# Weight preparation spread over more steps in a kernel that runs attention and a gated MLP side by side

## The chip, the cores and the metric

The kernel runs on one core of one Trainium2 chip. The core has five engines with queues of their own: TensorE (PE in the profile, with PEld for its weight loads), VectorE (DVE), ScalarE (ACT), GpSimd (POOL) and SyncE (SP, which here issues all DMAs). The metric is the device time of one execution in microseconds; the span in a profile goes from the first to the last instruction and is a little shorter.

## The reference

One block of a model on 2048 tokens of width 640. The layer-normed input goes two ways, and the product of the two is added to the input:

```python
def _A_ref(x, wqkv, wo):                  # sliding-window attention, H = 32 heads of 20, W = 256
    q, k, v = split(x @ wqkv)
    scores = einsum("bhqd,bhkd->bhqk", q, k) * (Dh ** -0.5)
    mask = (i - j >= 0) & (i - j < W)
    p = softmax(where(mask, scores, -1e9))
    return (p @ v).reshape(B, S, D) @ wo

def _B_ref(x, w1, b1, w2, b2):            # F = 1536
    h = x @ w1 + b1
    r = where(h > 0, h, 0)
    return (r * r) @ w2 + b2

xn = _layernorm(x)
return x + _A_ref(xn, wqkv, wo) * silu(_B_ref(xn, w1, b1, w2, b2))
```

(shortened; the shapes are x 2048x640, wqkv 640x1920, wo 640x640, w1 640x1536, w2 1536x640, all float32.)

## The kernel before

Every float32 factor of a dense product is split into two float16 parts, a high and a low one, after scaling by a power of two; a product is then three matmuls (high by high, high by low, low by high). To find the scale of a weight its squares are summed first. So each weight is loaded twice: once for squares (ACT, line 792, `unread<-raw`), once for the split, which takes one ACT instruction for the high part (line 126) and one DVE instruction for the low part (line 127).

The program has three parts. First, layer norm, transposes, the value product and the first group of 128 columns of q and k. Last, the product with wo, the gate and the residual. Between them lies the long middle part, to which nearly all of the change belongs: a loop over steps, written out by hand, so that each engine runs its instructions in the order in which the loop emits them.

A **step** of the middle part handles 128 queries of one pair of heads (16 pairs of 16 steps, 256 steps, and 13 more that only drain). In it stand, for different positions of a pipeline: `scores` (four matmuls into `sps`, line 574) and their running maxima on DVE (`junk`, line 585); ten steps later `scores_t` (four matmuls into `stps`, line 621), the exponential on ACT (`p`, line 626) and two masks on POOL (lines 627 and 629); one step later the high part of the probabilities on ACT (`ph`, line 634); one more step later the low part on DVE (`pl`, line 640); and at last 24 matmuls per two steps with the values (`ops`, line 654). There is a single PSUM tile for `stps`, so the next `scores_t` waits until the exponential has read the last one; likewise the next `scores` waits until the maxima have read both tiles of `sps`.

Into each step `fill` puts a fixed amount of **dense products**, reckoned in planned microseconds: 0.35 of it before and 0.65 of it after the middle of the step. The amount, `per`, is the planned total of 423.5 us divided by 268 steps, 1.58 us. The products come from a list of units:

- `group_unit`: q and k for groups 1 to 4 of 128 columns, 32 units of 15 matmuls of 512 columns (`qkps`, line 705), each evacuated by one ACT and one DVE instruction (lines 81 and 82);
- `hidden_unit`: the MLP's hidden layer, 96 units of 15 matmuls of 256 columns (`hps`, line 705), each evacuated by two ACT instructions (864 and 865), one on DVE (867) and one on POOL (868);
- `out_unit`: the MLP's second product, 96 units of 12 matmuls of 320 columns (`yps`, line 890); it needs w2 split.

The first 16 group units stand alone, the other 16 are merged with the 12 hidden units of the first block of 256 rows; then hidden units of one block and out units of the block before alternate.

The weights that the middle part prepares (q and k columns of the next group, the squares of w2 and wo, the splits of w2, the splits of wo) are **pieces** in one queue, first in, first out. `start_pieces` issues a piece's load on SP, at most three held at once; `release` emits its work on ACT and DVE, at most one piece a step, and not sooner than two steps after its load (`AGE`). `ensure` emits what is left of a kind at once. Evacuations are emitted by `flush` in the middle of a step.

## Time and profile before

| | |
|---|---|
| time, median of 3 runs (lowest to highest) | 834.24 us (833.88 to 835.12) |
| profiled execution: time, span | 834.25 us, 832.5 us |
| granted TensorE clock | 1.00 |
| PE, DVE, ACT, POOL busy | 815.6, 686.8, 646.7, 476.5 us |
| middle part: first `sps` matmul, last exponential | 117.2 us, 748.3 us |

Busy time of PE is to be read with care: a matmul's record lasts longer than the time after which the next can start (a record of 273 ns, but 15 matmuls in 1.64 us), so PE can look busy where it waits. What PE achieves is better read from counts: how many steps, four `sps` matmuls each, fall into a stretch of time. The records of DMA-issuing instructions show when SP issues them, not when the data lands.

### The profile page before, as it was taken

The numbers are of one execution on the slowest core, as the hardware profiler recorded it, in microseconds if no ns is written. First come the engines' busy times: TensorE is split into PE (matmuls) and PEld (weight loads), VectorE is DVE, ScalarE is ACT, GpSimd is POOL, SyncE is SP. The second block draws the span as 40 slices with busy tenths as digits, with TensorE's granted clock in tenths as the row PEclk, the third lists the DMA queues.
The fourth block names the chain that finished last, engine by engine and source line by source line (L and its number), as shares of the span: only waits on it lengthen the run. The fifth ranks groups of instructions, "written<-read, shape, count | busy, mean of one in ns | idle before, by whom it ended". The sixth has DMA issues, their size and how long they took to land.

```text
span 832.5 us, 24962 instructions
## 1 busy us (share of the span) xinstructions
PE 815.6 (98%) x9453; PEld 548.6 (66%) x9453; DVE 686.8 (82%) x1903; ACT 646.7 (78%) x1024; POOL 476.5 (57%) x874
## 2 busy tenths in 40 slices
PE   8999999999989999999999999999999999999998
PEld 7776553445555557777777777777777777767776
DVE  6777566788999889888988889888988889875665
ACT  4565446998898989898898989898898989893321
POOL 2000001456776778787877878787887878771000
PEclk9999999999999999999999999999999999999999
DMA  6895348765563332212121212212231231055883
GB/s 241 258 342 163 118 134 275 223 192 157 150 200 108 108 90 74 64 37 66 54 77 46 67 49 54 65 52 50 55 88 34 67 98 46 10 200 181 303 297 129
DMA packets 100641, 104.51 MB, mean 126 GB/s; under 512 B 42536, under 2 KB 73000, under 8 KB 100520
## 3 DMA queue, kind: packets, MB, share of 16 engines
q1 hardware_dynamic: 100520, 102.91, 40.4%
q8 instruction: 74, 1.21, 0.6%
q14 instruction: 47, 0.39, 0.2%
HBM read 65.67 MB, written 36.83 MB: 123 GB/s over the span
## 4 chain that ended last, share of the span: by engine, by line
PE 82%; ACT 7%; DVE 6%; issue 3%; DMA 2%; SPq 0%; DVEq 0%; ACTq 0%
PE hps L705 19%; PE yps L890 19%; PE wops L705 8%; PE ops L654 7%; PE qkps L705 7%; PE sps L574 7%; PE vps L293 6%; PE stps L621 3%; PE qkps L519 3%; ACT p L626 2%; DVE junk L585 1%; DVE pl L640 1%; ACT ph L634 1%; PE otp L972 1%; DMA raw<-in_B_w_dram 1%
## 5 line engine op out<-in xcount | busy, mean ns | idle before, releaser
L626 ACT ACTIVATE p<-stps,ebias,esc 128x768 f32<-128x768 f32 (+2 forms) x256 | 242.3, 946 | 50.0 <-PE stps L621 42.3
L585 DVE CUSTOM_DVE_ANT_0 junk<-sps,mask 128x320 bf16<-128x320 f32 (+2 forms) x512 | 221.5, 469 | 54.7 <-PE sps L574 44.3
L640 DVE TENSOR_TENSOR pl<-p,ph 128x768 f16<-128x768 f32 (+2 forms) x256 | 243.4, 951 | 4.8 <-ACT ph L634 4.1
L627 POOL TENSOR_SCALAR_AFFINE_SELECT p<-p 128x256 f32<-128x256 f32 x256 | 171.5, 670 | 90.4 <-ACT p L626 87.6
L634 ACT ACTIVATE ph<-p 128x768 f16<-128x768 f32 (+2 forms) x256 | 203.1, 793 | 2.1 <-POOL p L629 1.2
L705 PE MATMUL hps<-xT,w 128*128 128x256 f16 x1440 | 188.8, 273 | 0.0
L890 PE MATMUL yps<-w,hh 128*128 128x320 f16 x1152 | 186.6, 300 | 0.0
L705 PEld LDWEIGHTS <-w 128*128 128x128 f16 x1440 | 133.2, 98 | 43.7 <-issue 23.7
L890 PEld LDWEIGHTS <-hh 128*128 128x128 f16 x1152 | 105.1, 98 | 55.6 <-issue 21.8
L705 PE MATMUL qkps<-xT,qkw 128*128 128x512 f16 x480 | 117.0, 380 | 0.8 <-DVE w_t L154 0.8
L629 POOL TENSOR_SCALAR_AFFINE_SELECT p<-p 128x256 f32<-128x256 f32 x224 | 110.6, 494 | 0.0
L574 PE MATMUL sps<-ks,qs 60*64 60x320 f16 (+2 forms) x1024 | 86.0, 313 | 6.3 <-DVE mt L585 5.7
L654 PE MATMUL ops<-vp,ph 128*128 128x41 f16 x1440 | 89.8, 181 | 0.0
L654 PE MATMUL ops<-vp,pl 128*128 128x41 f16 x1440 | 89.5, 180 | 0.0
L654 PEld LDWEIGHTS <-ph 128*128 128x128 f16 x1440 | 84.5, 96 | 6.2 <-issue 0.6
L654 PEld LDWEIGHTS <-pl 128*128 128x128 f16 x1440 | 78.9, 96 | 5.8
L621 PE MATMUL stps<-qs,ks 62*64 62x320 f16 (+4 forms) x1024 | 79.6, 291 | 2.1 <-ACT p L626 1.8
L590 POOL CAST mp<-mt 128x8 f16<-128x8 f32 x64 | 44.0, 688 | 62.2 <-DVE mt L585 61.5
L705 PEld LDWEIGHTS <-qkw 128*128 128x128 f16 x480 | 41.6, 98 | 53.5 <-issue 11.7
L868 POOL TENSOR_TENSOR hh<-sq,hh 128x256 f16<-128x256 f32 x96 | 67.6, 704 | 13.0 <-DVE sq L867 9.3
L293 PE MATMUL vps<-wv,xT 128*128 128x320 f16 x480 | 69.6, 299 | 1.3 <-DVE xT L267 0.4
L705 PE MATMUL wops<-wo,oT 128*128 128x320 f16 (+1 forms) x495 | 66.7, 295 | 0.8 <-ACT oT L122 0.8
(152 smaller groups left out, 975.9 us busy)
## 6 DMA issues: line engine op xcount, KB each, us to landing
ks<-k_d SPq DMA_DIRECT2D x64, 120.0 KB
qs<-q_d SPq DMA_DIRECT2D x64, 120.0 KB
raw<-in_B_w_dram SPq DMA_DIRECT2D x24, 320.0 KB
v_d<-vt SPq DMA_DIRECT2D x8, 656.0 KB
vp<-v_d SPq DMA_DIRECT2D x16, 328.0 KB
xt<-in_A_x_dram SPq DMA_DIRECT2D x16, 320.0 KB
k_d<-shm SPq DMA_DIRECT2D x20, 256.0 KB
q_d<-shm SPq DMA_DIRECT2D x20, 256.0 KB
```

Of the source, the lines that this page charges most:

```text
L293: nc.tensor.matmul(ps, xT[b][:, xp, c, t * P:(t + 1) * P], wv[wp][:, c, nh * HALF:(nh + 1) * HALF], start=n == 0, stop=n == 3 * KC - 1)
L574: nc.tensor.matmul(ps[HB * j:HB * (j + 1), :nk], qs[i][rows_, q0:q0 + HB], ks[i][rows_, k0:k0 + nk], start=True, stop=True)
L585: nc.vector.tensor_tensor_reduce(out=junk[:, :nk], in0=ps[:, :nk], in1=mk, scale=1.0 / MAX_UNIT, scalar=-3.0e38, op0=ALU.add, op1=ALU.max, ...
L621: nc.tensor.matmul(ps[HB * j:HB * (j + 1), hh, c0:c1], ks[i][rows_, kb * P + HB * j:kb * P + HB * (j + 1)], qs[i][rows_, kb * P + c0:kb * ...
L626: nc.scalar.activation(p32[:, :, :n], ps[:, :, :n], AF.Exp, scale=esc[0], bias=ebias)
L627: nc.gpsimd.affine_select(p32[:, :, 0:P], p32[:, :, 0:P], pattern=[[0, 2], [1, P]], compare_op=ALU.is_ge, fill=0.0, base=0, channel_multip ...
L629: nc.gpsimd.affine_select(p32[:, :, 2 * P:], p32[:, :, 2 * P:], pattern=[[0, 2], [-1, P]], compare_op=ALU.is_gt, fill=0.0, base=0, channel ...
L634: nc.scalar.activation(ph[:, :, :n], p32[:, :, :n], AF.Copy)
L640: nc.vector.tensor_sub(pl[:, :, :n], p32[:, :, :n], ph[:, :, :n])
L654: nc.tensor.matmul(ot[:, q % 4, hh, :], t[:, hh, (q - k) * P:(q - k + 1) * P], vp[:, k // 4, k % 4, hh, :], start=m == 1, stop=m == 2 * le ...
L705: nc.tensor.matmul(ps, a, b_, start=j == 0, stop=j == n - 1)
L890: nc.tensor.matmul(ps, hh[:, hp, tt * P:(tt + 1) * P], lin1(w2t, (2 * fc + wp) * D + nh * HALF, HALF), start=fc == 0 and j == 0, stop=fc = ...
```

## The change

Seven edits, all in the order in which the middle part emits its work. The set of products, of their evacuations, of loads and of splits is the same.

1. **Pace.** `release` now also waits for a distance since the last piece of the same kind: 2 or 3 steps for splits of w2 (in turn), 2 steps for squares once the exponentials have begun (after step 11), 1 step for all else.
2. **Squares from the first unit on.** The 17 squares are queued when group 1 begins, not two units later. The loads for the next group of q and k are queued one unit later than before, and ahead of the squares that still wait in the queue; the `shut` flag that held them back is gone.
3. **12 per cent more dense products** in each of the first 72 steps: 1.77 planned us instead of 1.58; each later step gets 1.51, so that the total is the same.
4. **Merging begins earlier**: hidden units are mixed in after 12 group units, not 16.
5. **The scale of wo** is worked out by a function of its own, before the third hidden unit of the second block, not together with the scale of w2.
6. **The first turn moved**: the transposes of the first 256 rows of the attention's output (`otp`, then `oT`) are emitted before the last-but-one out unit, if their load has been issued, not after the last.
7. `transposes` is moved out of `out_filler` for that; its text is unchanged.

```diff
--- before.py
+++ after.py
@@ -734,6 +734,13 @@
     AGE = 2
     held = [0]
     shut = set()
+    last = {}
+
+    def pace(kind):
+        if kind == "2":
+            return 2 + len(w2t) % 2
+        return 2 if kind == "s" and state[2] > LAG + 1 else 1
+
 
     def start_pieces(n=3):
         k = 0
@@ -748,8 +755,9 @@
         done = []
         while started and len(done) < n:
             tag, at_, go = started[0]
-            if not force and (tag in shut or state[2] < at_ + AGE):
+            if not force and (tag in shut or state[2] < at_ + AGE or state[2] < last.get(tag[0], -9) + pace(tag[0])):
                 break
+            last[tag[0]] = state[2]
             done.append(started.pop(0)[2])
         return done
 
@@ -766,21 +774,24 @@
                 f()
                 held[0] -= 1
 
-    def piece(tag, src, go):
+    def piece(tag, src, go, ahead=False):
         def start():
             raw = wgt.tile([P, D], F32, tag="wraw", bufs=RAW, name="raw")
             if len(src.shape) == 3:
                 raw = raw.rearrange("p (c n) -> p c n", n=src.shape[-1])
             nc.sync.dma_start(raw, src)
             return lambda: go(raw)
-        queue.append((tag, start))
+        if ahead:
+            queue.insert(sum(t == tag for t, _ in queue), (tag, start))
+        else:
+            queue.append((tag, start))
 
     def queue_group(g):
         r = {}
         for i, w in enumerate("qk"):
             hi, lo = (qkw[0][:, g % 2, i, j] for j in range(2))
             off = (0 if w == "q" else D) + g * P
-            piece(f"g{g}", wqkv.rearrange("(c p) n -> p c n", p=P)[:, :, off:off + P], lambda raw, hi=hi, lo=lo, w=w: split_s(hi, lo, raw, sc_g[w]))
+            piece(f"g{g}", wqkv.rearrange("(c p) n -> p c n", p=P)[:, :, off:off + P], lambda raw, hi=hi, lo=lo, w=w: split_s(hi, lo, raw, sc_g[w]), True)
             r[w] = (hi, lo)
         return r
 
@@ -799,13 +810,16 @@
 
     def second_scales():
         s2, i2 = weight_scale("w2", totals("w2_t", pmm.tile([P, NF], F32, tag="mm", name="sums2"), mlp["g2"]))
-        so, io = weight_scale("wo", totals("wo_t", pmm.tile([P, KC], F32, tag="mm", name="sumso"), sso))
         sf = col("m_sf", NF)
         nc.vector.tensor_scalar(sf, mlp["ic2"], s2, None, ALU.mult)
+        mlp.update(s2=sf, i2=i2)
+
+    def out_scales():
+        so, io = weight_scale("wo", totals("wo_t", pmm.tile([P, KC], F32, tag="mm", name="sumso"), sso))
         iw = col("o_inv")
         nc.gpsimd.tensor_mul(iw, io, mlp["iv"])
         nc.gpsimd.tensor_scalar(iw, iw, 1.0 / (XS * V_DOWN), 1.0, ALU.mult, ALU.mult)
-        mlp.update(s2=sf, i2=i2, so=so, io=iw)
+        mlp.update(so=so, io=iw)
 
     w2t = []
 
@@ -826,17 +840,14 @@
         if w == "q":
             if b == 0:
                 ensure(f"g{g}")
-                if g + 1 < KC:
-                    ws[g + 1] = queue_group(g + 1)
-                    shut.add(f"g{g + 1}")
-            if b == 1:
-                shut.discard(f"g{g + 1}")
-                if g == 1:
-                    queue_squares()
-            if g == KC - 2 and b == 0:
+            if g == 1 and b == 0:
+                queue_squares()
+            if b == 1 and g + 1 < KC:
+                ws[g + 1] = queue_group(g + 1)
+            if g == 3 and b == 0:
                 ensure("s")
                 weighted_squares()
-            if g == KC - 2 and b == 1:
+            if g == 3 and b == 1:
                 second_scales()
                 for j in range(3):
                     queue_w2(j)
@@ -905,12 +916,14 @@
         groups = [(group_unit, g, b, w) for g in range(1, KC) for b in range(NB) for w in "qk"]
         hid = [[(hidden_unit, n, fc) for fc in range(NF)] for n in range(nblk)]
         mlp2 = [[(out_unit, n, tt, nh, third) for tt in range(2) for nh in range(2) for third in range(3)] for n in range(nblk)]
-        half = len(groups) // 2
-        units = groups[:half] + merge(groups[half:], hid[0])
+        first = 3 * NB
+        units = groups[:first] + merge(groups[first:], hid[0])
         for n in range(nblk - 1):
             units += merge(hid[n + 1], mlp2[n])
         units += mlp2[-1]
         for u in units:
+            if u == (hidden_unit, 1, 2):
+                out_scales()
             if u[:3] == (hidden_unit, nblk - 1, 0):
                 wo_part = queue_wo()
                 shut.add("o")
@@ -918,6 +931,8 @@
                 shut.discard("o")
                 load(0)
                 load(1)
+            if u == (out_unit, nblk - 1, 1, 1, 1) and 0 in ld:
+                yield from transposes(0)
             yield from u[0](*u[1:])
         ensure("o")
         yield from out_filler(wo_part)
@@ -947,34 +962,36 @@
             piece("o", wo[c * P:(c + 1) * P, :], lambda raw, hi=hi, lo=lo: split_s(hi, lo, raw, mlp["so"]))
         return lambda p, c: lin1(wob, (2 * c + p) * D, D)
 
+    oT = {}
+
+    def transposes(u):
+        ob = ld[u][0]
+        oT[u] = bigp.tile([P, SLOT], F16, tag="big", name=f"oT_{u}")[:, :SLOT // 2].rearrange("p (s c n) -> p s c n", s=2, c=KC)
+        for c0 in range(0, KC, 2):
+            cs = range(c0, min(c0 + 2, KC))
+            flush(mark() - 2)
+            if state[2] < 10 ** 6:
+                ps = pmm.tile([P, len(cs), MT], F32, tag="mm", name="otp")
+            else:
+                if c0 == 2:
+                    ps = pst.tile([P, 2, 4 * P], F32, tag="st", name="otp")[:, 0, :].rearrange("p (c n) -> p c n", n=MT)
+                else:
+                    ps = pat.tile([P, len(cs), MT], F32, tag="s", name="otp")
+            for c in cs:
+                for t in range(2):
+                    nc.tensor.transpose(ps[:, c - c0, t * P:(t + 1) * P], ob[:, t, c * P:(c + 1) * P], ident)
+                    yield 0.12
+
+            def evac(ps=ps, c0=c0, n=len(cs)):
+                split(oT[u][:, 0, c0:c0 + n], oT[u][:, 1, c0:c0 + n], ps)
+            pending.append(evac)
+
     def out_filler(wo_part):
-        oT, xts = {}, {}
+        xts = {}
 
         def load_res(t):
             xts[t] = wgt.tile([P, D], F32, tag="wraw", bufs=RAW, name="xres")
             nc.sync.dma_start(xts[t], x[t * P:(t + 1) * P, :])
-
-        def transposes(u):
-            ob = ld[u][0]
-            oT[u] = bigp.tile([P, SLOT], F16, tag="big", name=f"oT_{u}")[:, :SLOT // 2].rearrange("p (s c n) -> p s c n", s=2, c=KC)
...
 
         def finish(ps, sl, t2, nh, res, xt, t, yb):
             nc.vector.scalar_tensor_tensor(res[:, sl], ps, mlp["io"], yb[:, t2, sl], ALU.mult, ALU.mult)
@@ -1034,7 +1051,9 @@
                 return
             state[0] += c
 
-    per = total_ / (steps - 1)
+    first = 72
+    per_first = 1.12 * total_ / (steps - 1)
+    per_rest = (total_ - first * per_first) / (steps - 1 - first)
     with tc.manual_schedule(engines={E_.PE, E_.Activation, E_.DVE, E_.Pool, E_.SP}):
         exs, phs, norm, loads = {}, {}, [], []
 
@@ -1043,6 +1062,7 @@
 
         for s in range(steps):
             state[2] = s
+            per = per_first if s < first else per_rest
             post_all()
             issue(RATE)
             a, b, c, d, e = (at_step(s - lag) for lag in (0, LAG, LAG + 1, LAG + 2, LAG + 3))
```

What this does to the order of instructions shows on ACT, in the stretch in which squares stand between exponentials. Before (`p` is the exponential of a step, `ph` the high part, `unread` a square, `shm` the evacuation of a group unit):

```order
L626 ACTIVATE p_2007<-stps,ebias,esc 128x768
L792 ACTIVATE unread,ss_1588<-raw 128x640
L634 ACTIVATE ph<-p_1964 128x768
L626 ACTIVATE p_2054<-stps,ebias,esc 128x768
L81 ACTIVATE shm<-qkps 128x512
L792 ACTIVATE unread,ss_1588<-raw 128x640
L634 ACTIVATE ph<-p_2007 128x768
L626 ACTIVATE p_2093<-stps,ebias,esc 128x768
```

With the change:

```order
L626 ACTIVATE p_1951<-stps,ebias,esc 128x768
L634 ACTIVATE ph<-p_1910 128x768
L626 ACTIVATE p_1984<-stps,ebias,esc 128x768
L81 ACTIVATE shm<-qkps 128x512
L803 ACTIVATE unread,ss_1588<-raw 128x640
L634 ACTIVATE ph<-p_1951 128x768
L626 ACTIVATE p_2028<-stps,ebias,esc 128x768
L634 ACTIVATE ph<-p_1984 128x768
```

Every step had a square, from the 7th to the 23rd; now 8 squares come in the first 12 steps and 9 more in every second or third step up to the 31st.

On DVE, in the stretch of the splits of w2 (`w_0`), before:

```order
L640 TENSOR_TENSOR pl<-p_3448,ph 128x768
L127 SCALAR_TENSOR_TENSOR w_0_3464<-raw,m_sf,w_0_3464 128x640
L585 ISA junk,mt<-sps,mask 128x320
L585 ISA mt 128x1
L585 ISA junk,mt<-sps,mask 128x320
L585 ISA mt 128x1
L604 COPY mrow<-sps 16x128
L665 RECIPROCAL rs<-osb 128x8
L640 TENSOR_TENSOR pl<-p_3519,ph 128x768
L82 SCALAR_TENSOR_TENSOR shm<-qkps,shm 128x512
L127 SCALAR_TENSOR_TENSOR w_0_3464<-raw,m_sf,w_0_3464 128x640
```

With the change:

```order
L585 ISA junk,mt<-sps,mask 128x320
L585 ISA mt 128x1
L585 ISA junk,mt<-sps,mask 128x320
L585 ISA mt 128x1
L640 TENSOR_TENSOR pl<-p_3623,ph 128x768
L82 SCALAR_TENSOR_TENSOR shm<-qkps,shm 128x512
L585 ISA junk,mt<-sps,mask 128x320
L585 ISA mt 128x1
L585 ISA junk,mt<-sps,mask 128x320
L585 ISA mt 128x1
L640 TENSOR_TENSOR pl<-p_3699,ph 128x768
L127 SCALAR_TENSOR_TENSOR w_0_3483<-raw,m_sf,w_0_3483 128x640
```

The 12 splits stood in 12 steps running, steps 42 to 53; now they are spread over steps 41 to 70, with one or two steps without a split between two of them.

At the end of the middle part, on DVE, before (`oT` is the low part of the turned rows, `ysb` the evacuation of an out unit):

```order
L640 TENSOR_TENSOR pl<-p_15421,ph 128x2x256
L640 TENSOR_TENSOR pl<-p_15471,ph 128x2x128
L894 SCALAR_TENSOR_TENSOR ysb<-yps,w_i,b2t 128x320
L123 TENSOR_TENSOR oT_15552<-otp,oT_15552 128x512 x2
L123 TENSOR_TENSOR oT_15552<-otp,oT_15552 128x256
```

With the change:

```order
L640 TENSOR_TENSOR pl<-p_15423,ph 128x2x256
L123 TENSOR_TENSOR oT_15493<-otp,oT_15493 128x512
L640 TENSOR_TENSOR pl<-p_15473,ph 128x2x128
L123 TENSOR_TENSOR oT_15493<-otp,oT_15493 128x512
L123 TENSOR_TENSOR oT_15493<-otp,oT_15493 128x256
L905 SCALAR_TENSOR_TENSOR ysb<-yps,w_i,b2t 128x320
```

The turned rows are now read before the last `ysb`: while the three `otp` tiles are written, the last `yps` sum still holds one of the three PSUM tiles that they share, and the third `otp` tile takes the place of the first.

17 lines of the change are left out of this document (removed).

## The prediction

> **What bounds the kernel now.** I read the page first, then the middle part by stretches of whole steps, then the groups inside the two bad stretches, then the chain in a good one. The page:
>
> ```profile
> span 832.5 us, 24962 instructions
> PE 815.6 (98%) x9453; PEld 548.6 (66%) x9453; DVE 686.8 (82%) x1903; ACT 646.7 (78%) x1024; POOL 476.5 (57%) x874
> ```
>
> PE looks full throughout, but its records overlap, so its share doesn't say whether it waits. Counts do. The windows below hold only the `sps` matmuls of line 574, four to a step; the edges are put between steps, so 40 means ten steps:
>
> ```profile
> 117.10:137.50 20.40, 3.19 (x40) 1.00 0.73 228
> 137.50:170.70 33.20, 4.43 (x52) 1.00 0.83 254
> 170.70:195.50 24.80, 3.61 (x40) 1.00 0.51 150
> 195.50:215.80 20.30, 2.61 (x32) 1.00 0.51 146
> 215.80:253.00 37.20, 6.33 (x52) 1.00 0.62 184
> 253.00:296.40 43.40, 6.30 (x72) 1.00 0.37 104
> 361.80:713.20 351.40, 48.54 (x600) 1.00 0.22 59
> ```
>
> The last row is the calm state: 150 steps in 351.4 us, 2.343 us each. In the chain of waits two such steps look like this (start, length, what):
>
> ```profile
> 316.92 0.60 PE ops L654 x24
> 317.52 0.06 PE sps L600
> 317.58 0.23 PE sps L574 x4
> 317.81 0.14 PE stps L621 x4
> 317.95 0.24 PE yps L890
> 318.19 1.64 PE hps L705 x15
> ```
>
> PE follows PE without a gap: there the step is PE's own work, 15 `hps` matmuls taking 1.64 us where the planner reckons 15 x 0.111 = 1.665, a ratio of 0.985. So the planned 1.580 us of dense products in a step are 1.556 real ones. Against 2.343 the first 72 steps are slow. Ten of them (steps 0 to 9) have no `stps` and no `ops` yet: 2.343 less 0.24 (0.14, and 0.10 more for the product behind it) and less 0.30 (half of 0.60) is 1.80, and three more lack `ops`. What PE's work explains, what the rows show, and the loss:
>
> - steps 0-9: 18.0, 20.4, lost 2.4
> - 10-22: 13 x 2.343 - 0.9 = 29.6, 33.2, lost 3.6
> - 23-32: 23.4, 24.8, lost 1.4
> - 33-40: 18.7, 20.3, lost 1.6
> - 41-53: 30.5, 37.2, lost 6.7
> - 54-71: 42.2, 43.4, lost 1.2
>
> Together 16.9 us, 2 per cent of the span, and that is all there is to gain here. Who takes it? The same stretches with all engines (PE, PEld, DVE, ACT, POOL busy):
>
> ```profile
> 137.50:170.70 33.20, 30.74 (x307) 14.42 (x307) 25.03 (x77) 32.13 (x60) 14.25 (x34) 1.00 0.83 254
> 170.70:195.50 24.80, 24.19 (x271) 11.78 (x267) 22.14 (x62) 22.16 (x33) 14.20 (x30) 1.00 0.51 150
> 215.80:253.00 37.20, 33.43 (x370) 19.11 (x367) 36.95 (x90) 35.90 (x55) 28.57 (x42) 1.00 0.62 184
> 361.80:713.20 351.40, 351.40 (x4860) 252.66 (x4858) 313.18 (x921) 315.93 (x482) 285.56 (x504) 1.00 0.22 59
> ```
>
> In steps 10-22 ACT is busy 97 per cent, in steps 41-53 DVE 99 and ACT 97. In those stretches the step is theirs, not PE's. The groups (by shape) show what fills them, first in steps 10-22, then in 41-53:
>
> ```profile
> L792 ACT ACTIVATE unread<-raw 128x640 bf16<-128x640 f32 x14 | 10.4, 745 | 1.9 <-DMA raw<-in_B_w_dram 1.9
> L792 ACT ACTIVATION_READ_ACCUMULATOR unread<-raw 128x1 f32 x14 | 2.9, 208 | 0.0
> ```
>
> ```profile
> L127 DVE SCALAR_TENSOR_TENSOR w<-raw,m_sf,w 128x640 f16<-128x640 f32 x11 | 10.3, 937 | 0.0
> L126 ACT ACTIVATE w<-raw,m_sf 128x640 f16<-128x640 f32 x12 | 9.9, 821 | 0.0
> L81 ACT ACTIVATE shm<-qkps 128x512 f16<-128x512 f32 x5 | 2.9, 588 | 0.0
> L127 DVE SCALAR_TENSOR_TENSOR qkw<-raw,g_s,qkw 128x640 f16<-128x640 f32 x2 | 2.2, 1086 | 0.2 <-ACT qkw L126 0.2
> L864 ACT ACTIVATE relu<-hps,m,m 128x256 f32<-128x256 f32 x3 | 1.7, 568 | 0.0
> L126 ACT ACTIVATE qkw<-raw,g_s 128x640 f16<-128x640 f32 x2 | 1.6, 818 | 0.0
> L865 ACT ACTIVATE hh<-relu 128x256 f16<-128x256 f32 x3 | 1.2, 417 | 0.1
> ```
>
> One square a step, at most 0.745 + 0.208 = 0.95 us on ACT, and one split a step, 0.82 on ACT and 0.94 on DVE: these push a step from 2.343 to 2.55 (33.2 / 13) and 2.86 (37.2 / 13).
>
> **The change part by part.** *The splits of w2.* Without splits the stretch of steps 41-53 holds (36.95 - 10.3 - 2.2) / 13 = 1.88 us a step on DVE and (35.90 - 9.9 - 1.6) / 13 = 1.88 on ACT. Twelve splits over 30 steps add 0.4 x 0.94 = 0.38 and 0.4 x 0.82 = 0.33. The 12 per cent more dense work brings its evacuations: (2.9 + 1.7 + 1.2) / 13 x 0.12 = 0.05 on ACT, less on DVE. That makes 2.26 on either. PE's step grows by 0.12 x 1.556 = 0.187 to 2.530. PE becomes the bound with 0.27 to spare. I take 0.4 lost in steps 41-53 and 0.5 in 54-71, where splits now stand; none at best, half of today's loss at worst.
>
> *The squares.* Seven of them now fall into steps 10-22: 7 x 0.95 / 13 = 0.51 a step. The rest of ACT there lies between (32.13 - 10.4 - 2.9) / 13 = 1.45 (its pipeline still filling) and, from the next row, (22.16 - 2 x 0.82) / 10 = 2.05 (in part work left over from before). So 1.96 to 2.56 against 2.53: I take 0.6 lost. In steps 23-32 the earlier merge puts three hidden units (0.99 each), and four squares and two splits of q and k (0.82 each) are there too: up to 2.05 + (3.0 + 3.8 + 1.6) / 10 = 2.89, at least 2.3 with the lower base. This is the tightest place of the new order; 0.9 lost, 3.6 at worst.
>
> *The start.* Steps 0-9 lose 2.4 today, and the squares have a hand in it: ACT stands before them until their load lands (us in total, times, longest).
>
> ```profile
> ACT unread L792 <- DMA raw<-in_B_w_dram: 5.7, 4, 2.1
> ```
>
> Behind a waiting square, in ACT's order, stands the evacuation of the next group unit, and PE waits for its PSUM tile. Two loads of w2 now go out ahead of everything in the middle part, before the last stores of v, but six pieces still are loaded and used in the same crowded steps, two of them the splits of q and k, whose landing also holds DVE. A step of 0.187 more gives each load of two steps' age 0.4 us more. I take 2.0 left of 2.4 (between 1 and 3).
>
> *The scales.* Working out two scales together cost PE one wait:
>
> ```profile
> 212.32 1.24 PE L705 MATMUL qkps<-xT,qkw 128*128 128x512 f16 x5 [0.78 <-DVE w_t L154]
> ```
>
> Both sums held a PSUM tile of three; now each scale comes alone. Between no wait and 0.78 twice; I leave 0.4 for steps 33-40, this included. Losses left: 2.0 + 0.6 + 0.9 + 0.4 + 0.4 + 0.5 = 4.8 of 16.9, **a gain of 12.1**.
>
> *The dense work moved.* 72 x 0.187 = 13.4 us come into the first steps and leave the other 196, 0.068 each: 2.275 us. PE does the same work in all, so this is worth nothing by itself if the later steps follow. There ACT needs 315.93 / 150 = 2.11 a step, DVE 2.09, POOL 1.90: all below 2.275, ACT at 93 per cent instead of 90. I take 0.2 lost, 0 to 2.
>
> *The first turn.* Today:
>
> ```profile
> 753.51 1.25 PE L972 MATMUL otp<-ident,ob 128*128 128x128 f32 x10
> 755.52 0.30 PE L705 MATMUL wops<-wo,oT 128*128 128x320 f16 x1 [0.76 <-ACT oT L122]
> 754.15 1.36 ACT L122 ACTIVATE oT<-otp 128x512 f16<-128x512 f32 x3 [3.63 <-PE otp L972]
> 754.78 1.62 DVE L123 TENSOR_TENSOR oT<-otp,oT 128x512 f16<-128x512 f32 x3 [0.51 <-ACT oT L122]
> ```
>
> The 0.76 goes, since out units now cover the last of these evacuations. But the third `otp` tile has to wait for the first one's: the copy of two fifths of 1.36 (0.54) and the subtraction of two fifths of 1.62 (0.65), less the 0.44 in which PE writes the second tile, 0.75. An equal wait takes the place of the one removed. Behind it stand only out units, which nothing awaits. With five splits of wo in steps that are 0.068 shorter I count +0.2 for the end (-0.8 to +0.9).
>
> **The sum.** 834.25 (the profiled execution's own time; the median of the runs is 834.24) - 12.1 + 0.2 + 0.2 = **822.5 us**.
>
> **The rivals.** *Half of the loss stays.* ACT's and DVE's lateness in one step is carried into the next, and the losses of today also stand where the windows are not full (steps 23-32: ACT 89 per cent). If half of 16.9 stays, the time is 834.25 - 8.45 + 0.4 = 826.2. Against it: the calm row loses nothing at 90 per cent ACT. 13 per cent.
>
> *The later steps don't get shorter.* If POOL's chain between exponential and `ph` needs 2.343 a step, the 13.4 us moved into the early steps are paid in full: 834.25 - 12.1 + 13.4 + 0.2 = 835.7, no change by the bound below. For it: POOL's first select is slowed beside DVE, its second hardly, though the shape is one (rows of 320 to 720 us):
>
> ```profile
> L627 POOL TENSOR_SCALAR_AFFINE_SELECT p<-p 128x256 f32<-128x256 f32 x172 | 120.1, 698 | 47.4 <-ACT p L626 46.4 <-DVE rs L665 0.5
> L629 POOL TENSOR_SCALAR_AFFINE_SELECT p<-p 128x256 f32<-128x256 f32 x149 | 70.7, 475 | 0.0
> ```
>
> Against it: these busy times hold the slowing already, and still leave 0.37 us a step. 5 per cent. [...]
>
> *Slower.* ACT can't follow steps of 2.275, for it is the engine with the least room there: where a hidden unit falls, its evacuation comes on top, `stps` has one tile only, and PE then waits for the exponential. The gain of 11.9 is gone when each of the 196 later steps loses 0.061. Should they lose 0.14, as steps 23-32 do today with ACT at 89 per cent, it is 27.4 less the 0.2 in the sum: 849.7. Against it: 150 steps with the same hidden units lose nothing at 90. 4 per cent.
>
> **How the numbers follow.** The forecast has 78 per cent. The range reaches from nearly all of the loss gone with the bounds of the end (834.25 - 16.9 + 0.9 is 818.3) to beyond half of it left: 818.5 to 828.5; outside lie the last two rivals and some of the second. I call faster or slower what differs by over 0.2 per cent, 1.7 us, about what this kernel's runs can tell from no change. Forecast and first rival are both faster: 0.91; same 0.05; slower 0.04.
>
> **What would show it.** Right: the first 72 steps (288 `sps` matmuls) still take about as long as now, 162.4 + 13.4 + 4.8 = 180.6 us instead of 179.3, though they hold 13.4 us more of PE's work; no stretch with ACT or DVE over 97 per cent busy; 150 later steps in 341 us; the wait at `wops` gone and one before an `otp` of about as much. Wrong: the later steps still at 2.34, or ACT full in steps 23 to 32 with more than 2 us lost there.

## The result and the profile after

The changed kernel takes **823.85 us** (median of four runs, 823.25 to 825.52) against 834.68 us of the kernel before on the same chip (833.88 to 835.33): a ratio of **0.9874, 95 per cent interval 0.9856 to 0.9891**. The forecast was 822.5 us. The profiled execution of the changed kernel is the slowest of the four, 825.52 us.

The page, span and busy times:

```profile
span 823.8 us, 24953 instructions
PE 812.3 (99%) x9453; PEld 546.3 (66%) x9453; DVE 688.8 (84%) x1903; ACT 646.6 (78%) x1024; POOL 481.7 (58%) x874
```

As before, the busy share of PE says little, so the same stretches of whole steps are counted: steps 0-9, 10-22, 23-32, 33-40, 41-53, 54-71 and 100-249. The columns are the window, its length, the busy time of PE in the `sps` matmuls alone with their count (four to a step), the granted clock, the DMA share and GB/s:

```profile
117.50:140.90 23.40, 3.75 (x40) 1.00 0.76 237
140.90:172.70 31.80, 4.18 (x52) 1.00 0.75 225
172.70:198.00 25.30, 3.22 (x40) 1.00 0.53 155
198.00:218.60 20.60, 2.61 (x32) 1.00 0.47 138
218.60:253.50 34.90, 4.59 (x52) 1.00 0.60 172
253.50:299.40 45.90, 6.13 (x72) 1.00 0.46 136
363.80:705.00 341.20, 48.54 (x600) 1.00 0.22 59
```

PE's own work is 2.530 us a step in the first six rows (1.99 in steps 0-9, and 0.9 less over 10-22) and 2.275 in the last. What a row takes beyond it is the loss, as the prediction reckoned it. Throughout this document the losses are worked out so:

| steps | lost before | forecast | lost after |
|---|---|---|---|
| 0-9 | 2.4 | 2.0 | 3.5 |
| 10-22 | 3.6 | 0.6 | -0.2 |
| 23-32 | 1.4 | 0.9 | 0.0 |
| 33-40 | 1.6 | 0.4 | 0.4 |
| 41-53 | 6.7 | 0.4 | 2.0 |
| 54-71 | 1.2 | 0.5 | 0.4 |
| sum | 16.9 | 4.8 | 6.1 |

Four stages lose next to nothing now. The first ten steps lose more than before, and steps 41-53 keep 2.0. The 150 later steps take 341.2 us where 150 x 2.275 is 341.25: the work taken out of them is really gone from them.

The profiled run is 8.7 us shorter than the one before. By stages: the middle part begins 0.4 later; its first 72 steps take 181.9 us instead of 179.3 (+2.6); steps 72-99 take 64.4 instead of 65.4 (-1.0); steps 100-249 take 341.2 instead of 351.4 (-10.2); what follows takes 118.8 instead of 119.3 (-0.5). So the gain is seen in the later steps, and it is a gain because the 13.4 us of dense products that they gave up cost the early steps only 2.6.

The same windows with all engines (PE, PEld, DVE, ACT, POOL busy):

```profile
140.90:172.70 31.80, 31.80 (x319) 14.52 (x319) 26.66 (x76) 30.14 (x49) 16.97 (x36) 1.00 0.75 225
172.70:198.00 25.30, 25.30 (x302) 14.38 (x298) 21.96 (x63) 23.98 (x41) 15.36 (x31) 1.00 0.53 155
218.60:253.50 34.90, 33.57 (x380) 18.82 (x376) 32.02 (x88) 31.72 (x48) 24.04 (x41) 1.00 0.60 172
253.50:299.40 45.90, 45.90 (x539) 26.01 (x538) 43.96 (x119) 43.66 (x66) 35.91 (x57) 1.00 0.46 136
363.80:705.00 341.20, 341.20 (x4774) 244.25 (x4772) 313.02 (x918) 312.09 (x475) 286.31 (x502) 1.00 0.22 59
```

No stretch has ACT or DVE above 97 per cent any more; the fullest is DVE in steps 54-71 with 43.96 / 45.9, 96 per cent.

**Where the new losses lie.** Two places, one cause. ACT in steps 6 to 9 and in step 41 (timeline of ACT; start, length, what, in brackets the idle time before it and what ended it):

```profile
131.25 0.74 ACT L803 ACTIVATE unread<-raw 128x640 bf16<-128x640 f32 x1 [4.41 <-DMA raw<-in_B_w_dram]
133.54 0.83 ACT L126 ACTIVATE qkw<-raw,g_s 128x640 f16<-128x640 f32 x1 [0.97 <-DMA raw<-in_A_wqkv_dram]
135.90 0.83 ACT L126 ACTIVATE qkw<-raw,g_s 128x640 f16<-128x640 f32 x1 [1.54 <-DMA raw<-in_A_wqkv_dram]
219.74 0.83 ACT L126 ACTIVATE qkw<-raw,g_s 128x640 f16<-128x640 f32 x1 [2.03 <-DMA raw<-in_A_wqkv_dram]
```

The first two rows of `qkw` are the splits of group 2's q and k, which wait for their loads; the last row is the second split of group 4, at step 41. SP issued the loads of these three pieces at (timeline of SP):

```profile
128.96 0.38 SPq L782 DMA_DIRECT2D raw<-in_A_wqkv_dram  x1
130.99 0.40 SPq L782 DMA_DIRECT2D raw<-in_A_wqkv_dram  x1
214.51 0.51 SPq L782 DMA_DIRECT2D raw<-in_A_wqkv_dram  x1
```

From issue to the split that it releases are 4.6, 4.9 and 5.2 us. Two steps, the age at which a piece is used, are 5.06 us of PE's work, and 3.98 in the light steps of the start. Before, the loads of group 4 were issued at 199.17 and 200.30 us and its splits ran at 215.57 and 217.79: they had 16.4 and 17.5 us. The changed queue loads them when the second block of group 3 begins instead of the first, two group units later (the description of the change counts one), and the split stands in ACT's and DVE's order at step 41 whether its data is there or not. DVE waits behind ACT, and PE behind DVE's maxima. DVE in step 41:

```profile
220.60 0.88 DVE L127 SCALAR_TENSOR_TENSOR qkw<-raw,g_s,qkw 128x640 f16<-128x640 f32 x1 [1.43 <-ACT qkw L126]
```

PE at both places:

```profile
135.75 0.74 PE L574 MATMUL sps<-ks,qs 60*64 60x320 f16 x4 [1.18 <-DVE mt L585]
222.36 0.45 PE L574 MATMUL sps<-ks,qs 60*64 60x320 f16 x4 [1.12 <-DVE mt L585]
```

**The first turn.** PE in the end of the middle part:

```profile
740.47 0.60 PE L982 MATMUL otp<-ident,ob 128*128 128x128 f32 x4
741.28 0.66 PE L982 MATMUL otp<-ident,ob 128*128 128x128 f32 x4 [0.21 <-DVE ysb L905]
742.66 0.44 PE L982 MATMUL otp<-ident,ob 128*128 128x128 f32 x2 [0.72 <-DVE oT L123]
746.80 0.30 PE L705 MATMUL wops<-wo,oT 128*128 128x320 f16 x1
```

The 0.76 before `wops` is gone and 0.72 + 0.21 before the second and third `otp` tile have come.

**The scale of wo**, now alone, costs a wait of its own in step 74:

```profile
306.12 0.60 PE L705 MATMUL hps<-xT,w 128*128 128x256 f16 x4 [0.69 <-ACT relu L875]
```

`sumso` stands just ahead of this row on PE and has one of the three PSUM tiles; the hidden unit behind it waits until ACT has read another (line 875).

### The profile page after: what moved, and what is told of

Same layout as the page of the kernel before. It is cut to its first block, busy times and chain, and to the rows that moved or that the text cites. A ratio compares the mean times of both kernels' runs of the same rounds, so it can differ in the third digit from the quotient of the medians.

```text
span 823.8 us, 24953 instructions
## 1 busy us (share of the span) xinstructions
PE 812.3 (99%) x9453; PEld 546.3 (66%) x9453; DVE 688.8 (84%) x1903; ACT 646.6 (78%) x1024; POOL 481.7 (58%) x874
## 4 chain that ended last, share of the span: by engine, by line
PE 89%; ACT 4%; DVE 3%; DMA 2%; issue 1%; SPq 1%; POOL 0%; ACTq 0%; DVEq 0%; POOLq 0%
PE hps L705 20%; PE yps L901 19%; PE qkps L705 11%; PE ops L654 8%; PE wops L705 8%; PE sps L574 8%; PE vps L293 6%; PE stps L621 4%; PE qkps L519 3%; DMA raw<-in_A_wqkv_dram 1%; PE otp L982 1%; ACT p L626 1%; DMA wvr<-in_A_wqkv_dram 1%; PE tps L257 1%; ACT ph L634 1%
## 5 line engine op out<-in xcount | busy, mean ns | idle before, releaser
L574 PE MATMUL sps<-ks,qs 60*64 60x320 f16 (+2 forms) x1024 | 84.0, 313 | 2.6 <-DVE mt L585 2.3
L621 PE MATMUL stps<-qs,ks 62*64 62x320 f16 (+4 forms) x1024 | 77.5, 290 | 0.6 <-ACT p L626 0.4
```

Of the source, the lines that this page charges most:

```text
L574: nc.tensor.matmul(ps[HB * j:HB * (j + 1), :nk], qs[i][rows_, q0:q0 + HB], ks[i][rows_, k0:k0 + nk], start=True, stop=True)
L621: nc.tensor.matmul(ps[HB * j:HB * (j + 1), hh, c0:c1], ks[i][rows_, kb * P + HB * j:kb * P + HB * (j + 1)], qs[i][rows_, kb * P + c0:kb * ...
```

## The experiments

Theory: the early stages are bounded by ACT and DVE, so dense products put there are nearly free, and spreading the pieces brings ACT and DVE under PE's longer step; what is left is loads of q and k that are issued too late. The first rival is that one of the two, the spreading or the dense products, does it all alone; the second, that the later steps would soon stop following.

Losses by stage in the runs, worked out as above (PE's step is 2.343 where the 12 per cent are left out):

| run | us | 0-9 | 10-22 | 23-32 | 33-40 | 41-53 | 54-71 | sum |
|---|---|---|---|---|---|---|---|---|
| before | 834 | 2.4 | 3.6 | 1.4 | 1.6 | 6.7 | 1.2 | 16.9 |
| changed | 823.85 | 3.5 | -0.2 | 0.0 | 0.4 | 2.0 | 0.4 | 6.1 |
| pace alone | 833.12 | 1.6 | 1.6 | -0.1 | 5.0 | 3.3 | 3.4 | 14.8 |
| dense alone | 827.7 | 1.5 | 1.5 | 0.7 | 2.3 | 4.2 | 0.3 | 10.5 |
| changed, dense even | 831.53 | 6.6 | 0.0 | 0.7 | 0.2 | 4.2 | 3.9 | 15.6 |
| changed, w2 in every step | 827.47 | 3.5 | -0.2 | 0.0 | 0.4 | 4.2 | 0.2 | 8.1 |
| q, k wait three steps | 821.64 | 1.5 | -0.2 | 0.0 | 0.7 | 0.3 | 0.3 | 2.6 |
| the same, dense even | 828.21 | 2.7 | 0.4 | 0.7 | 0.3 | 3.8 | 2.8 | 10.7 |
| changed, old queue | 828.17 | 1.5 | -0.2 | 5.5 | 1.2 | 0.9 | 0.1 | 9.0 |

A single profile's stage is good to about half a microsecond where loads are awaited: the run with the old turn, whose first 250 steps are the changed kernel's word for word, lost 3.0 in steps 0-9 and 1.7 in 41-53.

**The pace alone**, put into the kernel before:

```diff
+    last = {}
+    def pace(kind):
+        if kind == "2":
+            return 2 + len(w2t) % 2
+        return 2 if kind == "s" and state[2] > LAG + 1 else 1
 ...
-            if not force and (tag in shut or state[2] < at_ + AGE):
+            if not force and (tag in shut or state[2] < at_ + AGE or state[2] < last.get(tag[0], -9) + pace(tag[0])):
 ...
+            last[tag[0]] = state[2]
```

> The kernel before with the pace of pieces alone (squares every second step after step 11, splits of w2 every 2 or 3 steps); no more dense work, no earlier squares, no earlier merge. Theory A (ACT and DVE set the pace where a piece stands in every step, and spreading pieces is what pays): steps 41 to 53 fall from 37.2 us to 31.5 to 32.5, steps 10 to 22 from 33.2 to about 31.5; behind them some loss comes back, since three pieces are forced out in step 33; about 827.5 us in all. Theory B (what pays is the dense work moved to the early steps, the pace only goes with it): 832 to 834 us.

Measured 833.12 us (831.76 to 833.91), ratio 0.9988 [0.9979, 0.9997]: next to nothing. Theory A's 827.5 did not come; the time is the one that theory B gives. Steps 41-53 lose 3.3 instead of 6.7, but the splits of w2 now stand in 54-71 too, which lose 3.4 instead of 1.2; in a step of 2.343 us there is no room for them anywhere. And a clump comes in: the squares, held back by the pace, stand ahead of group 3's pieces in the queue, and at step 33 the group's `ensure` emits all three at once. On PE:

```profile
194.10 0.60 PE L705 MATMUL qkps<-xT,qkw 128*128 128x512 f16 x2 [2.66 <-ACT qkw L126]
```

**The dense products alone**, put into the kernel before:

```diff
-    per = total_ / (steps - 1)
+    first = 72
+    per_first = 1.12 * total_ / (steps - 1)
+    per_rest = (total_ - first * per_first) / (steps - 1 - first)
 ...
+            per = per_first if s < first else per_rest
```

> The kernel before with 12 per cent more dense products in the first 72 steps alone. Theory A: where ACT and DVE need 2.55 and 2.86 us a step, a PE step of 2.53 fills their time: steps 10 to 22 stay at 33 to 34 us and steps 41 to 53 at 37 to 38.5, though each holds 2.4 us more of PE's work; the later 150 steps fall to 341 us. About 829 us. Theory B: 825 us or less.

Measured 827.7 us (827.44 to 828.33), ratio 0.9926 [0.9913, 0.994]. This one edit is worth 6.3 us by itself, more than half of the whole; it lies between theory A's 829 and theory B's 825. The first 72 steps take 186.2 us here instead of 179.3, so 6.9 of the 13.4 us moved are paid for. Steps 10-22 and 41-53 (all engines):

```profile
137.90:171.40 33.50, 32.48 (x320) 14.95 (x319) 27.00 (x75) 33.30 (x60) 15.14 (x35) 1.00 0.86 265
219.90:257.00 37.10, 34.25 (x381) 19.47 (x377) 36.17 (x93) 33.96 (x53) 27.70 (x41) 1.00 0.55 170
```

Both stages take what they took in the kernel before (33.2 and 37.2), with 13 x 0.187 = 2.4 us more of PE's work in each: ACT, at 33.30, sets the pace in the first and DVE, at 36.17, in the second, and PE's extra work costs nothing or next to it. The loss of these stages was not removed; it was filled.

**The changed kernel with the dense work even** again:

```diff
-    per_first = 1.12 * total_ / (steps - 1)
+    per_first = 1.0 * total_ / (steps - 1)
```

> The changed kernel with dense products spread evenly again (factor 1.00 for 1.12); pace, squares, merge, scales and turn as changed. Its profile has ACT at 2.32, 2.40, 2.44 and 2.43 us a step in steps 10-22, 23-32, 41-53 and 54-71, more than the 2.343 of PE's step without the additional work. Theory A: 0.1 us is lost in each of some 40 steps, 3 to 4 us: about 827.5 us. Theory B: nearly all of the gain goes, 831 to 834 us.

Measured 831.53 us (830.79 to 832.69), ratio 0.9973 [0.9962, 0.9983], again theory B's number and not A's 827.5. All the other edits together are worth some 2.4 us without it, though the first ten steps, told of at the end, lose 6.6 here. Steps 41-53 and 54-71:

```profile
213.60:248.30 34.70, 31.93 (x363) 17.40 (x359) 31.53 (x91) 29.85 (x45) 22.81 (x41) 1.00 0.57 170
248.30:294.40 46.10, 44.06 (x511) 24.39 (x511) 44.23 (x119) 42.15 (x64) 34.25 (x56) 1.00 0.49 141
```

In the second row DVE alone needs 44.23 / 18 = 2.46 us a step, more than PE's 2.343.

**The pieces of q and k wait three steps** instead of two:

```diff
-            if not force and (tag in shut or state[2] < at_ + AGE or ...
+            if not force and (tag in shut or state[2] < at_ + AGE + (tag[0] == "g") or ...
```

> The changed kernel with one number more: the splits of the q and k columns wait three steps after their load, not two. In the changed kernel's profile ACT waits for these loads 0.97 and 1.54 us at 133 to 136 us and 2.03 us at 218 us, DVE waits behind it, and PE loses 2.1 us in either place (134 to 138 and 221 to 226 us). Theory L (these losses are the landing of those loads, which takes about 5 us): both mostly go, 2 to 4 us off, 820 to 822 us. Rival (they are ACT's and DVE's lateness, and the wait for the load only where it shows): the waits move to the next piece, and the time stays within 1 us of 823.9.

Measured 821.64 us (821.23 to 821.99), ratio 0.9852 [0.9839, 0.9866]. Steps 0-9, then 41-53:

```profile
116.40:137.70 21.30, 21.30 (x125) 8.53 (x124) 14.21 (x53) 9.58 (x19) 0.79 (x4) 1.00 0.77 243
215.70:248.90 33.20, 33.20 (x381) 18.53 (x377) 31.88 (x88) 31.54 (x48) 25.13 (x42) 1.00 0.60 177
```

23.4 became 21.3 and 34.9 became 33.2, and no other row of the first 72 steps moved by more than 0.3: both new losses were the landing of these loads, 3.8 us in these two profiles. By the medians it is 2.2 (by the ratios 1.8), since the profiled run of the changed kernel is its slowest. The second split of group 4 now runs without a wait, a step later. In the start ACT still waits for the two loads of group 2, 1.09 and 1.06 us, but PE does not: the splits stand a step further back, and the maxima of the next step, for which PE waited, are now ahead of them in DVE's order. So the step more helps there by what no longer stands behind the late load, and not by making the load punctual. The wait of 4.41 us for a square's load, the first row of ACT shown for the changed kernel, has next to no share in the loss: it is still 4.03 here. That also settles what steps 41-53 lose for want of room on DVE and ACT: 0.3.

**The splits of w2 in every step** again, the rest as changed:

```diff
         if kind == "2":
-            return 2 + len(w2t) % 2
+            return 1
```

> The changed kernel with the splits of w2 let out one in each step again; dense work, squares, merge, scales and turn as changed. Theory S (slack and spreading need each other: in the changed kernel DVE has 2.44 to 2.46 us of work in a step of steps 41 to 71, just under PE's 2.53): with a split in each of 12 steps DVE needs some 2.18 + 0.87 = 3.0 a step there, steps 41 to 53 go from 34.9 to 38.5 to 40 us, and little comes back behind: 827 to 829 us. Rival (the additional dense work alone does it, and the pace is worth the 0.9 us that it brings to the kernel before): 824 to 825 us.

Measured 827.47 us (826.97 to 828.18), ratio 0.9925 [0.991, 0.9939] where the changed kernel has 0.9874: 3.6 us more by the medians, 2.0 by the stages of the two profiles. Steps 41-53:

```profile
218.00:255.10 37.10, 35.55 (x381) 19.96 (x377) 36.27 (x93) 36.62 (x56) 26.78 (x41) 1.00 0.66 201
```

ACT is busy 99 per cent and DVE 98, 2.85 us a step (3.0 were expected). So the spreading of w2 does pay once PE's step is long enough to spread into.

**Three steps and the dense work even**, both edits of above:

> The changed kernel with three steps for the q and k loads, and dense products spread evenly (factor 1.00). Without the additional work the changed kernel lost 6.6 us in steps 0 to 9 and 8.1 in steps 41 to 71. Theory S: what steps 41 to 71 lose is DVE's demand of 2.44 us against PE's 2.343, and stays: at least 0.1 in each of 31 steps and up to 8 us; steps 0 to 9 come down to 1.5 to 2 lost: 825.5 to 829 us. Rival (landing of loads in the shorter steps is the cause in both places): 822 to 824 us.

Measured 828.21 us (827.7 to 829.82), ratio 0.9931 [0.9914, 0.9947]. Against 821.64 with the 12 per cent, the dense work is worth 6.6 us also when the loads are in time. Here the parts can be put side by side: all but the dense work (called the spreading below, though queue, merge, scales and turn are in it) 0.9931, the dense work alone 0.9926, both 0.9852. In the whole they simply add up (5.8 + 6.2 us against 12.3). Not so by stages. In steps 10-32, where 5.0 were lost before, the spreading alone leaves 1.1 and the dense work alone 2.2, so either does most of it. In steps 41-71, where 7.9 were lost, the spreading alone leaves 6.6 and the dense work alone 4.5, and both together 0.6: 7.3 us saved, where the two alone save 1.3 and 3.4. There each needs the other for the rest.

**A quarter more instead of 12 per cent**, with the three steps:

```diff
-    per_first = 1.12 * total_ / (steps - 1)
+    per_first = 1.25 * total_ / (steps - 1)
```

> The changed kernel with three steps for the q and k loads and a factor of 1.25 for 1.12: 28 us of dense work moved, PE's step 2.73 us in the first 72 steps and 2.20 in the later ones. It asks for the point at which the later steps become too short: ACT has 2.07 us of work in them, 94 per cent. Theory S: the first steps have little left to give (2.6 us lost), and the later ones still run at PE's pace, 330 us for 150 steps: within 1.5 us of 821.6. Rival of the prediction (ACT's lateness in later steps): over 0.06 us lost in each, 832 us or more.

Measured 826.0 us (825.78 to 826.51), ratio 0.9907 [0.9893, 0.9922]; 4.4 slower than with 12, which is neither within the 1.5 us that I expected nor the rival's 832. Steps 54-71 and 100-249 (all engines):

```profile
260.20:311.60 51.40, 49.77 (x604) 32.27 (x602) 45.07 (x124) 44.08 (x68) 35.49 (x64) 1.00 0.34 99
373.20:704.60 331.40, 331.08 (x4682) 236.23 (x4680) 312.00 (x913) 307.95 (x469) 288.68 (x497) 1.00 0.22 61
```

A double split on ACT in the first of these rows:

```profile
288.70 1.53 ACT L126 ACTIVATE w<-raw,m_sf 128x640 f16<-128x640 f32 x2
```

PE's steps would be 2.73 and 2.20. The first row should take 49.2: 2.2 are lost, because units come so fast that the first out unit asks for w2 before its last pieces are through, and they are emitted together. The second should take 330.0 and loses 1.4, 0.009 a step. Behind step 250, where a split of wo stands in each of five steps, more is lost: that stretch takes 119.7 us instead of the 118.8 with 12 per cent, though 18 steps in it should be 0.074 shorter each. PE waits 1.79 us there for the exponential (`stps` at 724.32), and ACT, just before it, 1.22 us for POOL; what brings this about was not run apart. So 2.2 are lost at the end of the first steps, 1.4 in the 150 later ones and some 2.3 behind them. The 150 steps begin to show that they are near their limit, without a wall; behind them the shorter step does cost.

**The first turn with other PSUM tiles**, on top of the three steps: the first and third `otp` come from the pool of `sps` instead of that of `yps`, and splits of wo stand in every second step.

```diff
-                ps = pmm.tile([P, len(cs), MT], F32, tag="mm", name="otp")
+                ps = (pmm if c0 == 2 else pat).tile([P, len(cs), MT], F32, tag="mm" if c0 == 2 else "s", name="otp")
-        return 2 if kind == "s" and state[2] > LAG + 1 else 1
+        return 2 if kind == "o" or kind == "s" and state[2] > LAG + 1 else 1
```

> The changed kernel with three steps for the q and k loads, the first and third tile of the moved turn in the PSUM tiles that scores no longer need, and the splits of wo in every second step. In the changed kernel PE waits 0.21 and 0.72 us before the second and third tile by the rows (0.37 and 0.88 by the distance of the matmuls), and 0.9 in steps 256 to 260, where a split of wo stands in each. If these waits are PE's own and not covered, both go: 1.5 to 2 us under the 821.6 of the kernel with three steps, 819.5 to 820.5 us. If what follows only takes over the waits: 821.5 us.

Measured **819.34 us** (819.21 to 819.96), ratio 0.9828 [0.9813, 0.9843]. PE at the turn:

```profile
735.72 1.25 PE L982 MATMUL otp<-ident,ob 128*128 128x128 f32 x10
740.68 0.30 PE L705 MATMUL wops<-wo,oT 128*128 128x320 f16 x1
```

Ten transposes in a row without a wait. From the first `otp` to the first `wops` are 4.96 us instead of 6.33, 1.4 less. From step 250 to the first `otp` it is 0.9 less; that may be the splits of wo, but the two edits were not run apart.

**The old queue** in the changed kernel: squares two units later again, pieces of q and k queued early and behind the squares.

```diff
-            piece(f"g{g}", ..., True)
+            piece(f"g{g}", ...)
-            if g == 1 and b == 0:
-                queue_squares()
-            if b == 1 and g + 1 < KC:
-                ws[g + 1] = queue_group(g + 1)
+                if g + 1 < KC:
+                    ws[g + 1] = queue_group(g + 1)
+                    shut.add(f"g{g + 1}")
+            if b == 1:
+                shut.discard(f"g{g + 1}")
+                if g == 1:
+                    queue_squares()
```

> The changed kernel with one part undone: the squares start two units later again, and the pieces of q and k are queued early, behind the squares, instead of late and ahead of them. Theory (the start is slow because the loads of q and k go out late and among those of w2): steps 0 to 9 fall from 23.5 to 21.5 us; but at step 32 three pieces are then forced at once, as in the kernel with the pace alone, and steps 33 to 40 go from 20.6 to 23.5-25.5 us; the whole comes to 824 to 828. Rival (the start is slow because of the dense work alone, whatever the loads): steps 0 to 9 stay at 23.5 and the whole is over 826. Second rival: nothing moves, 823.9.

Measured 828.17 us (827.7 to 830.73), ratio 0.9934 [0.9914, 0.9954]. Steps 0-9 take 21.4, so the start's loss is the queue's order and not the dense work; and the clump is there, in step 32, which my rows count to 23-32 (I had put its price one row late). On PE:

```profile
197.96 1.96 PE L705 MATMUL qkps<-xT,qkw 128*128 128x512 f16 x4 [4.30 <-ACT qkw L126]
```

The window from just before the end of that wait on, all engines:

```profile
197.50:200.60 3.10, 2.64 (x29) 1.30 (x29) 1.68 (x2) 1.13 (x2) 0.00 (x0) 0.58 0.37 106
```

A wait of 4.30 us, and then a granted clock of 0.58. So the new order of the queue costs 2.0 us at the start and saves 5.5 here. Without it, all the other edits together are worth no more than the dense work alone (827.7 us).

**The old turn**:

```diff
-            if u == (out_unit, nblk - 1, 1, 1, 1) and 0 in ld:
-                yield from transposes(0)
```

> The changed kernel with the first turn put back behind the last out unit. If the new wait is as long as the old one, as predicted, 250 to the end stays at 115.2 +- 0.4 us and the time at 823.9 +- 0.6. Rival (the move is worth the old wait of 0.76, and the new one would have come anyhow): 824.6.

Measured 823.58 us (822.98 to 824.56), ratio 0.9872 [0.9854, 0.989]: no difference to the changed kernel. The old wait is back:

```profile
745.44 0.30 PE L705 MATMUL wops<-wo,oT 128*128 128x320 f16 x1 [0.76 <-ACT oT L122]
```

From step 250 to the start of the last matmul it takes 114.7 us, 0.4 less than with the turn moved (to the end of the span 118.3 instead of 118.8). The move by itself buys nothing. With other tiles, and the splits of wo in every second step, the same stretch was 2.3 us shorter than with the move alone; how much of that is the tiles' was not run apart.

**The old merge**, four groups of units first:

```diff
-        first = 3 * NB
+        first = 4 * NB
```

> The changed kernel with hidden units merged in from four groups of units on instead of three, as before the change. If ACT in steps 23 to 32 has room, as the trace of the changed kernel says (nothing lost there), the earlier merge bought nothing there; what changes is when the units of q and k ask for their pieces: earlier, so that a square is forced near step 29 and steps 23 to 32 lose 0.5 to 1.5 us: 823.5 to 825.5. Rival (the earlier merge is what makes room for the splits of w2 in steps 41 to 71): these lose 2 to 4 us more, 826 to 828.

Measured 824.23 us (823.78 to 824.78), ratio 0.9881 [0.9866, 0.9896]: no difference. Steps 23-32, 41-53 and 54-71 take 25.2, 33.8 and 46.4 us (25.3, 34.9 and 45.9 as changed). Neither the loss that I expected from a square forced near step 29 came, nor the rival's. By the medians the edit is neutral.

**wo's scale elsewhere**, on top of the turn with other tiles. By the edit it stands before the second out unit, one unit earlier than in the changed kernel (what was expected says the first):

```diff
-            if u == (hidden_unit, 1, 2):
+            if u == (out_unit, 0, 0, 0, 1):
```

> The fastest so far (q and k pieces wait three steps, first turn with other PSUM tiles) with wo's scale worked out before the first out unit instead of among the hidden units. If the 0.69 us that TensorE waits behind that scale comes from the PSUM tile it holds among hidden units, 818.6; if the wait only moves with it, 819.3.

Measured **818.22 us** (817.9 to 818.38), ratio **0.9808 [0.9793, 0.9823]**, the best of all. Steps 72-99 take 63.9 us instead of 64.8. The rows around `sumso`, on PE:

```profile
298.69 0.28 PE L152 MATMUL sumso<-ss_o,onesf 128*128 128x5 f32 x2
298.83 1.11 PE L901 MATMUL yps<-w,hh 128*128 128x320 f16 x7
300.96 0.60 PE L705 MATMUL hps<-xT,w 128*128 128x256 f16 x4
```

No unit behind it waits now. The out unit that follows (`yps`) goes on adding into a PSUM tile that the first out unit holds already, so it needs no new one, and the next hidden unit comes 2.3 us behind `sumso` instead of 1.0.

## Why the prediction was right, and where it was off

**The bound and the mechanism held.** The early steps were set by ACT and DVE, 16.9 us were lost there, and 10.8 of these are gone in the profiled run; 12.1 were forecast. "Half of the loss stays" would have left 8.45; 6.1 are left.

**The dense work moved: right.** Forecast were 341 us for the 150 later steps, 341.2 came. The two rivals in which the later steps don't follow both fall. The one that ends slower asked for 0.14 lost per later step; even at PE's step of 2.20, with a quarter more dense work in front, only 0.009 were lost in these 150 steps, though more behind them. I had said that moving this work "is worth nothing by itself if the later steps follow". That sentence was wrong: alone it made the kernel 6.3 us faster. Where a stage's step was set by another engine, PE's work put into it was free up to that engine's need: of the 13.4 us moved, 6.9 were paid in the first 72 steps and the rest was not. The sum had this gain, since it compared 2.530 with the other engines' need, but under the name of the spreading.

**The splits of w2: right in size, by errors that hid each other.** 0.4 was forecast for steps 41-53, and 0.3 are lost when the loads are in time. But I reckoned 2.26 us a step for DVE and so 0.27 to spare. Measured are 32.02 / 13 = 2.46 and 43.96 / 18 = 2.44, ACT 2.44 and 2.43: not 0.27 to spare but 0.09. I had taken the length of eleven records off a busy time in which records overlap (the split of the DVE row shown above is recorded with 0.88 us, and the next instruction starts 0.80 behind it), and so made the base too small. The row of steps 54-71 before, which holds only the last of the 12 splits, would have given it nearly straight:

```profile
253.00:296.40 43.40, 42.83 (x512) 23.78 (x511) 39.23 (x116) 38.33 (x57) 30.38 (x58) 1.00 0.37 104
```

39.23 / 18 = 2.18, and some 2.13 without that split, not 1.88; that the mix of units differs between the two stages has a share in this. With such a base the margin would have looked like next to none, and the forecast would have been worse: that it came out was in part luck. What the true figure tells is why the dense work and the spreading need each other in these steps: 2.44 does not fit under 2.343 and does fit under 2.530.

**The squares: better than forecast.** ACT needs 30.14 / 13 = 2.32 a step in 10-22 and 23.98 / 10 = 2.40 in 23-32; the first lies between the 1.96 and 2.56 that I had worked out, the second near the lower end of 2.3 to 2.89. Both are under 2.530, and both stages lose nothing where I left 0.6 and 0.9. "The tightest place of the new order" it was not.

**The start: the term that failed.** I left 2.0 (between 1 and 3); 3.5 came in the profiled run. I had priced the squares' loads and seen that q's and k's landing holds DVE, but then took the longer step as a help, "0.4 us more" of age. I didn't compare the age of two steps with the time a load takes there. It takes 4.6 to 5.2 us, and two steps there are 3.98 of PE's work. The same omission cost 1.7 in steps 41-53, where I had not looked for it at all: group 4's loads have 12 us less of lead than before.

**The scales: right at 33-40, missed at 74.** `sums2` alone costs nothing where it stands, and the stage loses the 0.4 forecast. `sumso` took its wait along: 0.69 in step 74, where I had put none.

**The first turn: right.** An equal wait was forecast, 0.75 in place of 0.76; 0.72 came before the third `otp`, and 0.21 before the second that I had not seen. Without the move the time is the same.

**The sum.** Against the profiled 825.52, the forecast of 822.5 is 3.0 short: 0.4 by which the middle part begins later, 1.3 in the first 72 steps (1.5 + 1.6 too little in the two stages with late loads, 1.8 too much in the others), 0.9 in steps 72-249, and 0.4 after them. Against the median it is 1.35 short.

## What to carry to other kernels

Where one engine's preparation work makes a stage longer than the main engine's own work, there are two remedies: move the main engine's work from other stages into it, which here cost next to nothing up to the other engine's need (steps 10-22 took 33.5 us instead of 33.2 with 2.4 us more of PE's work), and spread the preparation over more steps, which here helped only where those steps had room (next to nothing alone in steps of 2.343 us, 3.6 us for the splits of w2 in steps of 2.530); in the fullest stage here only both together did it. Before spreading, compare the need per step with the step, taking the need from a window that holds it and not by subtracting records; 0.1 us decided here (a need of 2.44 us against steps of 2.343 and 2.530). And when a queue is reordered, each load's lead must be set against its measured landing time (4.6 to 5.2 us here), and against what stands behind it in the engines' order: here 2.2 us were given back by loads that came a step late, and one number brought them back.

## What was not expected of the hardware

**The clock after a wait.** In the changed kernel with the dense work even, PE waited in the start and then ran at a lower granted clock. PE's rows:

```profile
136.72 0.22 PE L600 MATMUL sps<-identh,mp 128*128 128x128 f16 x1 [2.56 <-DVE mt L585]
137.39 3.80 PE L705 MATMUL qkps<-xT,qkw 128*128 128x512 f16 x9
```

The windows around them, all engines:

```profile
133.00:137.00 4.00, 1.44 (x8) 0.52 (x7) 1.63 (x6) 1.90 (x3) 0.00 (x0) 1.00 1.00 327
136.50:139.50 3.00, 2.78 (x11) 1.05 (x11) 2.92 (x11) 1.57 (x3) 0.00 (x0) 0.67 0.85 251
137.00:141.00 4.00, 4.00 (x13) 1.28 (x11) 2.42 (x9) 1.07 (x3) 0.00 (x0) 0.57 0.90 265
141.00:145.00 4.00, 4.00 (x31) 1.49 (x30) 2.42 (x9) 3.31 (x6) 0.96 (x3) 1.00 0.50 170
```

The nine `qkps` matmuls start 0.43 us apart, (3.80 - 0.38 for the record of one) / 8; elsewhere it is 0.22. Eight such distances are 1.7 us longer, which is part of the 6.6 lost there. The 0.67 and the 0.57 are means over the edges of a change. If the clock was at half in between, as 0.43 against 0.22 says, they put this time from about 137.5 to 141.0 us, an estimate. With the old queue a wait of 4.30 us was followed by a clock of 0.58 in the window shown there and of 0.88 in the one behind it (200.6 to 204.0 us); reckoned in the same way, that is half the clock from about 198.0 to 201.4. But with the pace alone a wait of 2.66 us, in the row shown there, was followed by matmuls 0.22 us apart (five in 1.25 us from 195.02 on), at full clock (1.00 from 190.4 to 214.0). So about the same wait, 2.56 and 2.66 us, was followed by the lower clock once and not another time; what decided it no run shows.

**Landing times.** The loads of 320 KB of q and k for which a split waited took 4.6 to 5.2 us from issue to use. In the window of the second of them the DMA engines were full, in that of the last they were not:

```profile
130.90:135.90 5.00, 3.82 (x21) 1.49 (x19) 2.89 (x9) 2.14 (x4) 0.00 (x0) 1.00 1.01 304
214.50:219.70 5.20, 5.20 (x64) 2.93 (x63) 4.67 (x10) 3.21 (x5) 2.47 (x6) 1.00 0.72 211
```

With a DMA share of 0.72 the load was no faster than with 1.01.
